# A constant table widened from 49 to 64 floats, so that every later tile in SBUF begins 32 bytes further on

## The chip, the cores and the metric

The kernel runs on one core of a Trainium2 chip. The metric is the device time of one execution in microseconds (us); the time before is the median of three runs. All data are 32-bit floats. The profile is one further execution, taken by the hardware profiler.

The engines are TensorE (PE in the profile; PEld is its loading of weights), VectorE (DVE), ScalarE (ACT), GpSimd (POOL) and SyncE (SP), which here only issues transfers. Transfers run on 16 DMA engines that all queues share.

## The reference

```python
# x: (8, 3136, 256); filt_r, filt_i: (1569, 256)
X = np.fft.rfft(x, axis=1)
Y = X * (filt_r + 1j * filt_i)[None]
y = np.fft.irfft(Y, n=3136, axis=1).astype(np.float32)

h  = y.reshape(25088, 256) @ w_in                  # (25088, 1024)
e  = np.exp(h - np.max(h, axis=-1, keepdims=True))
solu = h * (e / (np.sum(e, axis=-1, keepdims=True) + 1e-9))
mu  = np.mean(solu, axis=-1, keepdims=True)
var = np.mean((solu - mu) ** 2, axis=-1, keepdims=True)
out = ((solu - mu) / np.sqrt(var + 1e-6) * g_ln) @ w_out   # (25088, 256)
```

A filter is applied to each of the 8 batch elements along the sequence by a Fourier transform there and back; then every token goes through a feed-forward block.

## The kernel before

The Fourier transform is made of matrix products in two steps there (49 by 64 points) and two steps back. The last step back uses the table `wb_t`. The intermediate results go through DRAM, since each step needs another order of the rows. Batch element 0 is transformed first; those of elements 1 to 7 run beside the feed-forward blocks of the elements before them.

The constants are allocated one after another, ahead of all working tiles:

```python
wf_t = consts.tile([NR, NK], FP32, name="wf_t")          # 100 floats per partition
wq_t = consts.tile([P, 2, 64], FP32, name="wq_t")        # 128
wi_t = consts.tile([NK, NR], FP32, name="wi_t")          # 98
wb_t = consts.tile([P, N1], FP32, name="wb_t")           # N1 = 49
w_in_sb = consts.tile([P, 7, DFF // 2], FP32, name="w_in_sb")
w_out_sb = consts.tile([P, 7, KF // 2, C // 2], FP32, name="w_out_sb")
...
y = consts.tile([P, KD, PAIR], FP32, name="y")
```

The allocator rounds each tile's bytes per partition up to a multiple of 32. The program before places them so (bytes from the start of a partition):

| tile | begins at | past a multiple of 64 | past a multiple of 512 |
|---|---|---|---|
| wf_t | 16512 | 0 | 128 |
| wq_t | 16928 | 32 | 32 |
| wi_t | 17440 | 32 | 32 |
| wb_t | 17856 | 0 | 448 |
| w_in_sb | 18080 | 32 | 160 |
| w_out_sb | 32416 | 32 | 160 |
| y | 46816 | 32 | 224 |
| turn (two buffers) | 97760, 114144 | 32 | 480 |
| solu_t (four buffers) | 144864 to 157152 | 32 | 480 |
| u, s, h, e, x, t2, t4, f, g, de and the other working tiles | 101856 to 225760 | 32 | 480 |

The small tiles of one to four floats (nmax, esum, rsum and the like) lie 32 bytes apart and alternate between 0 and 32 past a multiple of 64.

The use of the table: 64 products per piece of a batch element, each with a small result of 64 x 49.

```python
def back_halves(e, ch, pss):
    ...
    nc.tensor.matmul(out=views[g][64 * h:64 * h + 64, cb, i, :],        # line 367
                     lhsT=t4[rows, i, c0:c0 + 64], rhs=wb_t[rows],
                     start=True, stop=True)
```

Its load, once: `nc.gpsimd.dma_start(out=wb_t, in_=wb_dram)`.

The feed-forward part works on pairs of blocks of 128 tokens. Each of its two products is done with seven block products in place of eight, from sums and differences of blocks (lines 717 and 829; GpSimd forms the sums, line 696):

```python
nc.tensor.matmul(out=ms[j, bank], lhsT=lhsT, rhs=w_in_sb[:, w, :], ...)          # 717: 128x128 by 128x512
...
for f in range(KF // 2):
    nc.tensor.matmul(out=pos[p, bank], lhsT=lhs[:, f, :], rhs=w[:, f, :], ...)   # 829: 128x128 by 128x128
```

Between the two products the activations must be transposed. VectorE transposes squares of 32 x 32, and transfers from SBUF to SBUF put the squares in place:

```python
def turn(k):
    g, i = divmod(k, 4)
    if i == 0:
        turns[g] = wk2.tile([P, DFF // 32, 4, 32], FP32, name=f"turn_{g}", tag="turn")
    nc.vector.transpose(out=turns[g][:, :, i, :], in_=...)                # line 775

def regroup(p, i):
    turned = turns[g].rearrange("p (k q) b i -> p k q (b i)", q=4)
    a = 2 * second + i
    st = upool.tile([P, KF, P], FP32, name=f"solu_t_{p}_{i}", tag=f"solu_t{i}")
    for q in range(4):
        nc.sync.dma_start(out=st[32 * q:32 * q + 32, :, :],               # line 787
                          in_=turned[32 * a:32 * a + 32, :, q, :])
```

Each of these 784 transfers moves 128 KB from 32 partitions to 32 others, in runs of 512 bytes: 4 x 32 floats that stand together in `turn`, 2048 bytes apart, and go to 8 neighbouring places of 512 bytes in `solu_t`.

Of the kernel before, what the change touches and what calls it, by code (L numbers as in the profile page):

```python
# [9 lines left out]
FP32 = mybir.dt.float32  # L10
# [7 lines left out]
P = 128  # L18
# [5 lines left out]
N1, N2 = 49, 64  # L24
# [70 lines left out]
def kernel(  # L95
# [10 lines left out]
    nc = tc.nc  # L106
# [4 lines left out]
    wb_dram = nc.inline_tensor(wb_host, name="wb_tbl").ap()  # L111
    de_dram = nc.inline_tensor(de_host, name="de_tbl").ap()

    def pool(name, bufs, space=None, stack=ctx):
        kw = {} if space is None else {"space": space}
        return stack.enter_context(tc.tile_pool(name=name, bufs=bufs, **kw))

    consts = pool("consts", 1)
# [8 lines left out]
    wf_t = consts.tile([NR, NK], FP32, name="wf_t")  # L127
    wq_t = consts.tile([P, 2, 64], FP32, name="wq_t")
    wi_t = consts.tile([NK, NR], FP32, name="wi_t")
    wb_t = consts.tile([P, N1], FP32, name="wb_t")  # L130


    w_in_sb = consts.tile([P, 7, DFF // 2], FP32, name="w_in_sb")
# [222 lines left out]
    def back_halves(e, ch, pss):  # L356

        t4 = t4s.pop((e, ch))
        views = [ps.rearrange("p a c -> p (a c)")[:, 0:KD * NCH * N1].rearrange(
            "p (c i r) -> p c i r", c=KD, i=NCH) for ps in pss]  # L360
        for cb in range(KD):
            for i in range(NCH):
                for g in range(2):
                    rows = slice(64 * g, 64 * g + NK // 2)
                    for h in range(2):
                        c0 = cb * P + 64 * h
                        nc.tensor.matmul(out=views[g][64 * h:64 * h + 64, cb, i, :],  # L367
                                         lhsT=t4[rows, i, c0:c0 + 64], rhs=wb_t[rows],
                                         start=True, stop=True)
        even = t4.rearrange("p i c -> p (i c)")[:, 0:KD * NCH * N1]  # L370
        even = even.rearrange("p (c r i) -> p c r i", c=KD, i=NCH)
        nc.scalar.copy(out=even, in_=views[0].rearrange("p c i r -> p c r i"))
        joins[e, ch] = even, views[1].rearrange("p c i r -> p c r i")
# [23 lines left out]
    with ExitStack() as st:  # L397
# [92 lines left out]
        def begin(j):  # L490
            raws[j] = load_words(weights[j][1], j)
# [35 lines left out]
        def idle(out):  # L527

            nc.tensor.matmul(out=out, lhsT=tables[0][0][:, 0, 0].rearrange("p u q -> p (u q)"),
                             rhs=filters[0][0][:, 0], start=True, stop=True)  # L530
# [13 lines left out]
        def start(i):  # L544
            sp.fetch_filter(i)
            sp.fetch_de(i)
            sp.forward(i, halves(f"pb_0_{i}"))
# [4 lines left out]
        for n in range(16):  # L552
            (nc.sync, nc.scalar)[n % 2].dma_start(
                out=t2_0[NH * (n % 4):NH * (n % 4) + NH, n // 4, :], in_=rows_x[n:n + 1])
# [6 lines left out]
        for i in range(units):  # L561
            if i + 2 < units:
                start(i + 2)
            sp.multiply(i, 0, nc.vector.tensor_tensor)
            sp.multiply(i, 1, nc.gpsimd.tensor_tensor)
            pss = [ps_t.tile([P, 2, C], FP32, name=f"pc_0_{i}_{u}", tag="t") for u in range(2)]
            idle(pss[0])
            sp.inverse(i, pss)
            sp.store(i, nc.scalar.dma_start)
            if i == 0:  # L570
                nc.gpsimd.dma_start(out=wi_t, in_=wi_dram)
                nc.gpsimd.dma_start(out=wq_t, in_=wq_dram)
                nc.gpsimd.dma_start(out=wb_t, in_=wb_dram)
                nc.gpsimd.dma_start(out=g_sb, in_=moe_g_ln.rearrange("(k p) -> p k", p=P))
            elif i != 2:
                begin({1: 2, 3: 3, 4: 4, 5: 5, 6: 6}[i])
# [7 lines left out]
        for i0, n, rows in ((0, 4, P), (4, 4, P), (8, NP - 9, P), (NP - 1, 1, NQ)):  # L584
            f, at = filters[i0]
            nc.sync.dma_start(
                out=f_dram[i0:i0 + n].rearrange("i u q k c -> (u q) i (k c)")[0:rows],
                in_=f[0:rows, at:at + n].rearrange("p i k c -> p i (k c)"))
# [279 lines left out]
    for e in range(1, B):  # L868
# [42 lines left out]
        for ch, t in enumerate(back_at):  # L911
            row_loads.append((
                t, t - 1, spectrum_at[-1] + 2, lambda e=e, ch=ch: fetch_back(e, ch)))
            second_one = ch and t == back_at[ch - 1]
            (late if second_one else early)[t].append(lambda e=e, ch=ch: back_halves(
                e, ch, [psum(f"py_{e}_{ch}_{g}") for g in range(2)]))
            (late if second_one else middle)[t].append(lambda e=e, ch=ch: join_halves(e, ch))
# [136 lines left out]
```

## Time and profile before

| | before |
|---|---|
| time, median of 3 runs | 1713.54 us (1708.46 to 1720.54) |
| span of the profiled run | 1710.7 us |
| TensorE busy | 1574.3 us, 92% |
| VectorE busy | 1288.1 us, 75% |
| GpSimd busy | 1139.1 us, 67% |
| ScalarE busy | 904.5 us, 53% |
| moved by DMA | 312.12 MB in 377,805 packets |
| of these on SyncE's queue (q1) | 306,260 packets, 169.81 MB, 47.0% of 16 engines' time |
| packets of 512 bytes (solu_t<-turn) | 200,704, mean 43.3 ns |

How to read it: busy time is that in which an engine has an instruction at work; matrix products are pipelined and their ends are modelled, so a busy TensorE need not be at its peak. The granted clock of TensorE is 0.98 of full speed over the span. The DMA share is the mean of 16 engines. A chain of waits is followed back from the last instruction: at each step to what released it, or to the instruction before it on its engine. The records of single packets have a size, a start and a duration, and no address; the packets of 512 bytes on SyncE's queue are all of the transfer solu_t<-turn, since 784 x 256 = 200,704.

### The profile page before, as it was taken

To read this page: it belongs to the slowest core of one execution; us is meant where nothing else is said; L and a number is where in the kernel's file an instruction comes from. 1 tells how busy PE (TensorE), PEld (TensorE's weight loads), DVE (VectorE), ACT (ScalarE), POOL (GpSimd) and SP (SyncE) were. 2 spreads that over 40 slices of the span, in tenths; PEclk is the share of its full clock that TensorE was granted. 3 is DMA by queue.
4 is the path that set the end of the run, shared out by engine and by line. 5 is a ranking of instruction groups with operands and counts; after the bars stand their busy time and mean duration, and the time that the engine had idled before them with its cause. 6 is when DMAs were issued, how large, how long until landed. Compare 5 with 4: busy or idle time off the path is not lost.

```text
span 1710.7 us, 36871 instructions
## 1 busy us (share of the span) xinstructions
PE 1574.3 (92%) x12710; PEld 1048.9 (61%) x12710; DVE 1288.1 (75%) x2633; ACT 904.5 (53%) x1772; POOL 1139.1 (67%) x1325
## 2 busy tenths in 40 slices
PE   5798899899899999999998999899999999999996
PEld 1353356666656666666665676566666777777776
DVE  1586777887787878887887779777888777777772
ACT  2145454456455555565555654455555565666662
POOL 4444886677766776688567865577757676676664
PEclk8899899999999999999999999999999999999999
DMA  9888878987898779877888779867896666655554
GB/s 248 234 251 233 231 198 200 232 203 178 193 221 215 184 172 225 214 185 168 209 210 206 175 173 210 196 173 166 189 218 172 119 128 123 116 108 103 112 108 96
DMA packets 377805, 312.12 MB, mean 182 GB/s; under 512 B 63322, under 2 KB 343395, under 8 KB 377619
## 3 DMA queue, kind: packets, MB, share of 16 engines
q1 hardware_dynamic: 306260, 169.81, 47.0%
q0 software_dynamic: 34464, 101.68, 21.1%
q10 hardware_dynamic: 36896, 38.28, 8.1%
q8 instruction: 102, 1.67, 0.4%
q14 instruction: 83, 0.68, 0.1%
HBM read 124.86 MB, written 81.50 MB: 121 GB/s over the span
## 4 chain that ended last, share of the span: by engine, by line
PE 54%; DMA 25%; DVE 9%; SPq 4%; issue 4%; ACT 2%; POOL 2%; ACTq 0%; DVEq 0%; POOLq 0%
PE m L717 23%; PE o L829 22%; DMA solu_t<-turn 11%; DMA de<-de_tbl 3%; DMA x<-in_x_dram 3%; SPq L787 3%; PE py L367 3%; DVE h L765 2%; DMA out_dram<-ot 2%; PE pa L221 2%; PE pb L296 1%; DVE turn L775 1%; PE pa L264 1%; DMA rs_t<-rows 1%; PE pc L296 1%
## 5 line engine op out<-in xcount | busy, mean ns | idle before, releaser
L829 PE MATMUL o<-w_out_sb,solu_t 128*128 128x128 f32 x3136 | 402.3, 277 | 38.6 <-DVE rsum L760 36.8
L829 PEld LDWEIGHTS o<-w_out_sb,solu_t 128*128 128x128 f32 x3136 | 380.9, 192 | 89.7 <-DVE rsum L760 43.7
L767 ACT ACTIVATE e<-h,nmu 128x1024 f32<-128x1024 f32 x196 | 224.6, 1146 | 385.6 <-DVE h L765 385.5
L717 PE MATMUL m<-w_in_sb,s 128*128 128x512 f32 x784 | 396.3, 607 | 15.5 <-ACT h L727 13.7
L696 POOL TENSOR_TENSOR u<-solu_t 128x512 f32<-128x512 f32 x98 | 145.4, 1483 | 385.6 <-DMA solu_t<-turn 280.6
L829 PEld LDWEIGHTS o<-w_out_sb,u 128*128 128x128 f32 x2352 | 303.8, 192 | 155.0 <-issue 101.1
L717 PE MATMUL m<-w_in_sb,y 128*128 128x512 f32 x588 | 315.4, 620 | 14.5 <-DVE nmax L741 6.7
L829 PE MATMUL o<-w_out_sb,u 128*128 128x128 f32 x2352 | 315.3, 277 | 9.2 <-ACT ot L841 9.1
L765 DVE SCALAR_TENSOR_TENSOR h<-e,rsum,h 128x1024 f32<-128x1024 f32 x196 | 291.6, 1488 | 6.9
L727 ACT COPY h<-m 128x512 f32<-128x512 f32 x294 | 173.6, 591 | 207.6 <-PE m L717 172.9
L845 DVE SCALAR_TENSOR_TENSOR ot<-o,rs_t,ot 128x128 f32<-128x128 f32 x294 | 100.5, 342 | 199.1 <-ACT ot L841 134.2
L775 DVE STREAM_TRANSPOSE turn<-h 128x1024 f32<-128x1024 f32 x196 | 242.7, 1238 | 0.1
L749 ACT ACTIVATE e<-h,nmax 128x1024 f32<-128x1024 f32 x196 | 226.3, 1155 | 0.0
L741 DVE CUSTOM_DVE_ANT_0 h<-m,h 128x512 f32<-128x512 f32 x196 | 134.7, 687 | 116.8 <-ACT h L727 96.3
L717 PEld LDWEIGHTS m<-w_in_sb,s 128*128 128x128 f32 x784 | 128.3, 191 | 104.1 <-issue 69.4
L841 ACT ACTIVATE ot<-o,rs_t 128x128 f32<-128x128 f32 x392 | 142.9, 365 | 71.8 <-PE o L829 63.3
L696 POOL TENSOR_TENSOR u<-solu_t,u 128x512 f32<-128x512 f32 x98 | 143.2, 1461 | 43.4 <-PE o L829 38.1
L717 PEld LDWEIGHTS m<-w_in_sb,y 128*128 128x128 f32 x588 | 96.8, 193 | 119.7 <-DVE nmax L741 42.2
L696 POOL TENSOR_TENSOR u<-u,solu_t 128x512 f32<-128x512 f32 x98 | 142.3, 1452 | 0.6
L696 POOL TENSOR_TENSOR solu_t<-solu_t,solu_t 128x512 f32<-128x512 f32 x98 | 136.9, 1397 | 7.7
L696 POOL TENSOR_TENSOR s<-y 128x128 f32<-128x128 f32 x196 | 103.8, 530 | 1.0
L367 PEld LDWEIGHTS py<-wb_t,t 50*64 50x64 f32 x3584 | 57.8, 134 | 43.7 <-PE o L829 14.4
(113 smaller groups left out, 1969.6 us busy)
## 6 DMA issues: line engine op xcount, KB each, us to landing
solu_t<-turn SPq DMA_DIRECT2D x784, 128.0 KB
out_dram<-ot SPq DMA_DIRECT2D x196, 128.0 KB
t<-d POOLq DMA_DIRECT2D x112, 200.0 KB, 5.0
d<-x POOLq DMA_DIRECT2D x100, 200.0 KB, 6.4
f<-f_dram POOLq DMA_DIRECT2D x39, 512.0 KB, 8.6
d<-g POOLq DMA_DIRECT2D x39, 512.0 KB, 5.8
t<-d ACTq DMA_DIRECT2D x36, 512.0 KB
x<-in_x_dram SPq DMA_DIRECT2D x112, 98.0 KB
```

What stands on the lines that cost most here:

```text
L367: nc.tensor.matmul(out=views[g][64 * h:64 * h + 64, cb, i, :], lhsT=t4[rows, i, c0:c0 + 64], rhs=wb_t[rows], start=True, stop=True)
L696: nc.gpsimd.tensor_tensor(out=out, in0=in0, in1=in1, op=op)
L717: nc.tensor.matmul(out=ms[j, bank], lhsT=lhsT, rhs=w_in_sb[:, w, :], start=m in (1, 2, 7), stop=True, skip_group_check=True)
L727: nc.scalar.copy(out=h_half(k, i), in_=ms[j, 0])
L741: nc.vector.tensor_tensor_reduce(out=h_half(k, i), in0=ms[j, bank], in1=h_half(*kept), scale=1.0, scalar=sofar, op0=ALU.add, op1=ALU.min, ...
L749: nc.scalar.activation(out=e, in_=hs[k], func=AFT.Exp, bias=nmaxs.pop(k)[:, 1:2], scale=-1.0, accum_out=esum)
L765: nc.vector.scalar_tensor_tensor(out=solu, in0=e, scalar=rsum, in1=solu, op0=ALU.mult, op1=ALU.mult, accum_out=nmu)
L767: nc.scalar.activation(out=e, in_=solu, func=AFT.Square, bias=nmu, scale=-float(DFF), accum_out=variances[g][:, i:i + 1])
L775: nc.vector.transpose(out=turns[g][:, :, i, :], in_=solus.pop(k).rearrange("p (f j) -> p f j", j=32))
L829: nc.tensor.matmul(out=pos[p, bank], lhsT=lhs[:, f, :], rhs=w[:, f, :], start=f == 0 and m in (1, 2, 7), stop=True, skip_group_check=True)
L841: nc.scalar.activation(out=out_half(p, *to)[0], in_=pos[p, 0], func=AFT.Copy, scale=rs)
L845: nc.vector.scalar_tensor_tensor(out=ot, in0=pos[p, bank], scalar=rs, in1=out_half(p, *kept)[0], op0=ALU.mult, op1=ALU.add)
```

## The change

`wb_t` becomes 64 floats wide. The product and the load use the first 49 columns as before. The aim is the place of all that is allocated after it: with 256 bytes in place of 224, every later tile moves up by 32 bytes, so that all large tiles begin at multiples of 64 bytes, and the working tiles, the transposed ones among them, at multiples of 512.

```diff
-    wb_t = consts.tile([P, N1], FP32, name="wb_t")
+    wb_t = consts.tile([P, 64], FP32, name="wb_t")
...
-                                         lhsT=t4[rows, i, c0:c0 + 64], rhs=wb_t[rows],
+                                         lhsT=t4[rows, i, c0:c0 + 64], rhs=wb_t[rows, 0:N1],
                                          start=True, stop=True)
...
-                nc.gpsimd.dma_start(out=wb_t, in_=wb_dram)
+                nc.gpsimd.dma_start(out=wb_t[:, 0:N1], in_=wb_dram)
```

## The prediction

> **What bounds the kernel now.** I read the page's 40 slices first, then the windows by stage, the chain that ended last, the waits, and last the records of single DMA packets. The change moves addresses, and an address is something that a transfer or an engine's operand may feel. The slices say how full TensorE and the transfers are, in tenths:
>
> ```profile
> PE   5798899899899999999998999899999999999996
> DMA  9888878987898779877888779867896666655554
> ```
>
> The windows by stage give the same in microseconds (the columns after the length are PE, PEld, DVE, ACT and POOL busy, then granted clock, DMA share, GB/s):
>
> ```profile
> 200.00:1310.00 1110.00, 1036.54 (x9311) 698.58 (x9311) 895.32 (x1790) 604.94 (x1214) 775.83 (x915) 1.00 0.82 197
> 1310.00:1500.00 190.00, 187.54 (x1526) 133.61 (x1525) 143.19 (x323) 113.52 (x223) 130.99 (x150) 1.00 0.62 123
> 1500.00:1600.00 100.00, 100.00 (x565) 71.54 (x564) 74.45 (x171) 62.48 (x123) 68.91 (x72) 1.00 0.56 108
> ```
>
> So there are two regimes. From 200 to 1310 us the Fourier steps of later batch elements run beside the feed-forward blocks: the 16 DMA engines are 82% busy and TensorE has 1110 - 1036.5 = 73 us of gaps. From 1310 us TensorE is full and the transfers are at 56 to 62%. In that last stage the chain runs through TensorE alone; this is one turn of it, one pair of blocks (14 products of line 717, 56 of line 829, and among the pieces left out the 64 small ones of line 367, 1.08 us):
>
> ```profile
> 1401.89 1.78 PE o L829 x16
> 1403.68 1.72 PE m L717 x4
> 1405.39 1.78 PE o L829 x16
> 1407.18 1.72 PE m L717 x4
> 1408.90 1.78 PE o L829 x16
> ...
> 1415.52 1.78 PE o L829 x16
> ```
>
> It takes 1415.52 - 1401.89 = 13.63 us and nothing but TensorE's own work is in it. No transfer can shorten this stage. The shares of the whole chain, by engine and by line:
>
> ```profile
> PE 54%; DMA 25%; DVE 9%; SPq 4%; issue 4%; ACT 2%; POOL 2%; ACTq 0%; DVEq 0%; POOLq 0%
> PE m L717 23%; PE o L829 22%; DMA solu_t<-turn 11%; DMA de<-de_tbl 3%; DMA x<-in_x_dram 3%; SPq L787 3%; PE py L367 3%; DVE h L765 2%; DMA out_dram<-ot 2%; PE pa L221 2%; PE pb L296 1%; DVE turn L775 1%; PE pa L264 1%; DMA rs_t<-rows 1%; PE pc L296 1%
> ```
>
> And the longest wait for a transfer (us in total, times, longest):
>
> ```profile
> POOL u L696 <- DMA solu_t<-turn: 280.6, 74, 11.0
> ```
>
> The transfer solu_t<-turn (the regrouping of the transposed activations, SBUF to SBUF) is the one that matters: 11.2% of the chain by the unrounded answer, 191 us, its long pieces all before 1310 us, where it stands in a queue with the loads and stores of the Fourier steps. GpSimd waits 280.6 us for it in all, then forms the sums that line 829 multiplies.
>
> [...]
>
> [...] The trace does not show such a penalty plainly. The 16-byte packets of rs_t<-rows read 16-byte rows of which most are off such multiples, and 5,454 of the 6,272 take just 9 ns. And packet times by size (the shortest common value) are 27 ns for 512 bytes, 46 for 1024, 84 for 2048, 159 for 4096: a line of (159 - 46) / 3072 = 0.0368 ns a byte plus 8.3 ns. [...] packets of 4 to 16 bytes take 7 to 9 ns too, so it is rather a fixed cost of any packet.
>
> [...] of the 200,704 packets of 512 bytes, 24% take at most 29 ns and half take 40 to 52 ns, with a median of 44 and a mean of 43.3. [...]
>
> [...]
>
> **The change part by part.** wb_t grows from 49 to 64 floats, from 196 to 256 bytes. The allocator rounds to 32 bytes, so it took 224: everything allocated later moves up by 32 bytes, no more. solu_t goes from 144864 to 144896, which is 283 x 512; turn from 97760 to 97792, 191 x 512; y from 46816 to 46848, 32 past a multiple of 64 to a multiple of 64.
>
> Removed: nothing. Added: nothing. The product of line 367 reads the first 49 of 64 columns in wb_t, one contiguous run as before, so its 3,584 pairs at 134 and about 17 ns stay. The one load of wb_t writes the same rows. No instruction, wait or queue order changes; only what the hardware makes of the addresses can.
>
> The operand that may gain is the 512-byte packet. Its sum is 200,704 x 43.3 ns / 16 engines = 543 us of all engines, of which 361 us fall between 200 and 1310 us, where all packets together take 913. Three outcomes:
>
> (a) No address effect: packets stay at 43.3 ns, nothing moves. Time 1713 plus or minus the spread of the runs (1708.46 to 1720.54).
>
> (b) A small effect: [...] a saving of 3 to 4 ns is plausible, 8% (chosen, not derived). On the path: 8% of the chain's 191 us = 15 us. Elsewhere: 8% of 361 = 29 us less work of 913 in the shared stage, 3%, which shortens the queueing of the other chained transfers (25% of 1711 = 428 us, less 191, is 237 us) by up to 3%, 7 us. Of the 22 us I expect part to be lost, since TensorE takes over wherever it catches up: some 15 us. Time about 1698.
>
> (c) The full estimate: each packet falls to near its floor, 43.3 to 31 ns, 28%. On the path 0.28 x 191 = 53 us; the others 0.28 x 361 / 913 = 11% of 237 = 26 us. Together 79, but TensorE has only 73 us of gaps in the shared stage and not all belong to this wait; perhaps 50 us with what the start gives. Time about 1663.
>
> **The rivals.** Rival one is (a), that 32 past a multiple of 64 costs nothing: for it speak the 9 ns packets, the line through the sizes[...]. [...] Rival two: the transfers do get faster but the end does not, because TensorE is the bound. For it: 92% busy, and the last 400 us run on TensorE alone. Against: GpSimd's 280.6 us of waiting and 25% of the chain in transfers before 1310 us. It would put the time at 1705 to 1713. Rival three: the engines feel 64-byte lines, GpSimd above all, since its sums of 128x512 take 1277 ns (median of u<-solu_t) and hold VectorE up (line 765 takes 1285 ns at the median and up to 2510). A few per cent off these would be worth 5 to 10 us. Nothing in the profile speaks for it but the round number. Rival four, slower: all work tiles now start at the same place within 512 bytes, but they did before too, at 480, so I see no new collision; a changed order of arrivals may cost a few microseconds.
>
> **Range and chances.** I give (a) with rivals two to four 55%, centred on 1712; (b) 33%, on 1698; (c) 12%, on 1663. The mean is 0.55 x 1712 + 0.33 x 1698 + 0.12 x 1663 = 1701.5; the middle of the distribution lies a little higher, so I say 1704. Faster by over 2% means below 1679.3: nearly all of (c) and a little of (b), 0.16. Slower by over 2%, above 1747.8, has no mechanism: 0.03. The rest, 0.81, within 2%. Eight times in ten: 1670 to 1720.
>
> **What would show it.** Right: the 512-byte packets' mean at 39 to 43 ns, DMA share between 200 and 1310 us at 0.79 to 0.82, the wait of GpSimd for solu_t<-turn at 250 to 280 us, and the late turn at 13.63 us still. If packets fall below 35 ns, (c) holds and the DMA share should drop to about 0.73. If packets stay and GpSimd's 1277 ns or TensorE's 13.63 us change, it was the engines' side. [...]

## The result and the profile after

The kernel after takes 1694.69 us (median of 4 runs, 1693.12 to 1697.80), the kernel before 1713.92 beside it. The ratio is 0.9888, 95% interval 0.985 to 0.9926: 1.1% faster.

The slices of the kernel after, TensorE and transfers:

```profile
PE   5897899999989999999989999999999999999996
DMA  9886868776788678666886668766883544344343
```

and its windows, with the same columns as before:

```profile
200.00:1310.00 1110.00, 1055.35 (x9448) 715.07 (x9449) 909.47 (x1837) 618.69 (x1241) 788.85 (x934) 1.00 0.73 199
1310.00:1500.00 190.00, 182.57 (x1476) 129.74 (x1475) 141.80 (x305) 110.41 (x216) 124.14 (x141) 1.00 0.45 113
1500.00:1600.00 100.00, 96.59 (x544) 68.70 (x543) 76.29 (x166) 59.68 (x117) 64.56 (x68) 1.00 0.41 104
```

Two things happened. Up to 1310 us the DMA share fell from 0.82 to 0.73 while slightly more bytes were moved per second (197 to 199 GB/s), and TensorE's gaps shrank from 73 to 55 us. After 1310 us the transfers have even more room (0.62 to 0.45, 0.56 to 0.41), and there TensorE, full before, now has gaps: 2.5 us of 190 became 7.4, and 0 of 100 became 3.4.

The packets of 512 bytes (all of solu_t<-turn) went from a mean of 43.3 to 33.0 ns. GpSimd's wait for that transfer, 280.6 us before, and the chain of the kernel after:

```profile
POOL u L696 <- DMA solu_t<-turn: 146.2, 43, 7.7
```

```profile
PE 53%; DMA 19%; DVE 15%; issue 4%; POOL 4%; SPq 3%; ACT 1%; ACTq 0%; DVEq 0%; POOLq 0%
```

Transfers fell from 25% of the chain to 19%, but VectorE rose from 9% to 15%. Where that sits is seen in the chain of the kernel after in the last stage, which before was TensorE alone (start, length, what):

```profile
1500.50 1.16 DVE turn L775
...
1502.19 2.38 DVE h L765 x2
1504.57 0.68 DVE h L738 x2
...
1505.30 1.13 PE m L717 x2
1506.42 0.95 PE o L829 x8
```

In most turns TensorE now waits for VectorE: for line 738, which empties the PSUM bank that the next product needs and which stands behind a line 765 of 2.38 us with its accumulator read. The waits from 1310 to 1600 us (us in total, times, longest), first of the kernel before, then of the kernel after:

```profile
PE m L717 <- DVE h L738: 1.1, 2, 0.7
```

```profile
PE m L717 <- DVE h L738: 10.8, 17, 0.9
```

A clock for both kernels is the start of chosen products of line 717 in the profiled runs (1372 products of 128x512 in all; numbers count from 0):

| | first product, us | from there to product 980 | from 980 to the last | rest | span |
|---|---|---|---|---|---|
| before | 113.7 | 1186.1 | 362.2 | 48.8 | 1710.7 |
| after | 107.7 | 1157.4 | 380.0 | 50.9 | 1695.9 |
| difference | -6.1 | -28.7 | +17.8 | +2.1 | -14.8 |

So 35 us were gained by product 980 and 18 given back after it. The third column is called the shared stage below, the fourth the last stage.

### The profile page after: what moved, and what is told of

Read it like the earlier page. It is cut to its first block, busy times and chain, and to the rows that moved or that the text cites. A ratio compares the mean times of both kernels' runs of the same rounds, so it can differ in the third digit from the quotient of the medians.

```text
span 1695.9 us, 36871 instructions
## 1 busy us (share of the span) xinstructions
PE 1568.3 (92%) x12710; PEld 1050.2 (62%) x12710; DVE 1299.2 (77%) x2633; ACT 904.1 (53%) x1772; POOL 1136.0 (67%) x1325
## 4 chain that ended last, share of the span: by engine, by line
PE 53%; DMA 19%; DVE 15%; issue 4%; POOL 4%; SPq 3%; ACT 1%; ACTq 0%; DVEq 0%; POOLq 0%
PE m L717 21%; PE o L829 21%; DMA solu_t<-turn 11%; DVE h L765 5%; PE py L367 3%; DVE turn L775 3%; SPq L787 3%; PE pb L296 2%; PE pa L264 2%; DMA x<-in_x_dram 2%; DVE h L738 2%; PE pc L296 1%; DVE ot L845 1%; DMA d<-x 1%; DMA rows<-rs 1%
## 5 line engine op out<-in xcount | busy, mean ns | idle before, releaser
L696 POOL TENSOR_TENSOR u<-solu_t 128x512 f32<-128x512 f32 x98 | 131.7, 1344 | 308.1 <-DMA solu_t<-turn 146.2
L765 DVE SCALAR_TENSOR_TENSOR h<-e,rsum,h 128x1024 f32<-128x1024 f32 x196 | 302.3, 1542 | 6.9
L741 DVE CUSTOM_DVE_ANT_0 h<-m,h 128x512 f32<-128x512 f32 x196 | 134.8, 688 | 113.7 <-ACT h L727 93.0
L717 PEld LDWEIGHTS m<-w_in_sb,y 128*128 128x128 f32 x588 | 96.0, 191 | 128.7 <-DVE h L738 44.5
L696 POOL TENSOR_TENSOR solu_t<-solu_t,solu_t 128x512 f32<-128x512 f32 x98 | 153.4, 1565 | 7.7
L367 PEld LDWEIGHTS py<-wb_t,t 50*64 50x64 f32 x3584 | 57.6, 134 | 42.9 <-PE o L829 14.4
```

The source lines that it names most:

```text
L696: nc.gpsimd.tensor_tensor(out=out, in0=in0, in1=in1, op=op)
L741: nc.vector.tensor_tensor_reduce(out=h_half(k, i), in0=ms[j, bank], in1=h_half(*kept), scale=1.0, scalar=sofar, op0=ALU.add, op1=ALU.min, ...
L765: nc.vector.scalar_tensor_tensor(out=solu, in0=e, scalar=rsum, in1=solu, op0=ALU.mult, op1=ALU.mult, accum_out=nmu)
```

## The experiments

All were timed beside the kernel before, whose medians in the three sets were 1717.20, 1716.43 and 1717.07 us; the ratios refer to these. "Shared" packets are those of 512 bytes between 200 and 1250 us, "late" ones those from 1400 us on. For these two, and for the start of product 980 in experiments 9 and 10, time counts from the trace's zero, which lies 10.4 to 10.8 us ahead of the span's start; all other times count from the span's start. Shared stage and last stage are as in the table above, from one profile each. The three profiles in which nothing but GpSimd's own tiles or the order of late sums differs from the kernel before agree within 6.3 us in the shared stage (1183.4 to 1189.7), so a difference of a few microseconds between two profiles there is not read.

### 1. src_only: the destination off its place again

```diff
 # the kernel after
+    pad_a = pool("pad_a", 1).tile([P, 8], FP32, name="pad_a")
     upool = pool("up", 2)
+    pad_b = pool("pad_b", 1).tile([P, 120], FP32, name="pad_b")
```

> The kernel after, but solu_t (and u1, s14 beside it) 32 bytes further on: the source turn still starts at a multiple of 512, the destination solu_t is 32 past one. Theory R (the read side pays[...]): packets of 512 bytes stay at 33 ns as in the kernel after, time about 1695 us. Theory W (the write side pays[...]): packets go back to 43 ns, time about 1713. Theory L (both ends pay alike): about 38 ns, time about 1700.

Measured: 1708.33 us, ratio 0.9951 (0.9928 to 0.9974). Packets 35.4 ns in all, 36.5 shared, 32.3 late (after: 33.0, 33.3, 32.1). Shared stage 1165.0, last stage 378.7. The read end sets the late packets: with the source in place they take 32.1 ns with the destination in place too and 32.3 with it off. Where the transfers are busier (DMA share 0.77 from 200 to 1250 us in this run, 0.42 from 1400 to 1600) the write end shows too, 36.5 for 33.3.

### 2. dst_only: the destination alone in its place

```diff
 # the kernel before, with the same two pads
+    pad_a = pool("pad_a", 1).tile([P, 8], FP32, name="pad_a")
     upool = pool("up", 2)
+    pad_b = pool("pad_b", 1).tile([P, 120], FP32, name="pad_b")
```

> The kernel before, but solu_t (and u1, s14 beside it) 32 bytes further on: the destination starts at a multiple of 512, the source turn stays at 480 past one. Theory R: packets stay at 43 ns, time about 1713 us. Theory W: packets fall to 33 ns, time about 1695. Theory L: about 38 ns, time about 1703.

Measured: 1695.48 us, ratio 0.9877 (0.9843 to 0.9912). Packets 41.6 in all, 40.5 shared, 44.3 late (before: 43.3, 42.9, 44.6). Theory R was right on the packets (they hardly change) and wrong on the time: the whole 1.2% is there. Shared stage 1165.8, and the last stage stays at 362.4, as in the kernel before. So the time does not follow the packets of this transfer.

### 3. past64 and past256: which multiple matters

```diff
-    wb_t = consts.tile([P, 64], FP32, name="wb_t")
+    wb_t = consts.tile([P, 80], FP32, name="wb_t")     # past64; 128 for past256
```

> The kernel after with the table 80 floats wide: every later tile 64 bytes further on, so turn and solu_t are 64 past a multiple of 512: a multiple of 64, not of 256. If multiples of 64 are what matters: packets 33 ns, time 1695 us, no difference from the kernel after. If multiples of 256 or 512 matter[...]: 36 to 43 ns, time 1700 to 1713.

> The kernel after with the table 128 floats wide: every later tile 256 bytes further on, so turn and solu_t are 256 past a multiple of 512. If multiples of 64 or of 256 are what matters: packets 33 ns, time 1695 us. If a run may not cross a multiple of 512: 38 to 43 ns, time 1705 to 1713.

Measured: past64 1706.38 us, ratio 0.9924 (0.9886 to 0.9963), packets 37.3 in all and 36.0 late, shared stage 1177.3, last 363.4. past256 1694.25 us, ratio 0.9858 (0.9824 to 0.9892), packets 33.1 and 32.2, shared stage 1153.6, last 377.9. A multiple of 64 is not enough, and 512 is not needed; a multiple of 256 does all that the change does.

### 4. after_wait_late: why the last stage became slower

VectorE's line 765 (the normalising product) and GpSimd's sums of line 696 start near each other in every turn. In the kernel before (timeline, start and length in us):

```profile
1550.87 1.28 DVE L765 SCALAR_TENSOR_TENSOR h<-e,rsum,h 128x1024 f32<-128x1024 f32 x1
1551.22 2.07 POOL L696 TENSOR_TENSOR u<-solu_t 128x512 f32<-128x512 f32 x1 [2.45 <-DMA solu_t<-turn]
```

and in the kernel after:

```profile
1528.75 1.27 POOL L696 TENSOR_TENSOR u<-solu_t 128x512 f32<-128x512 f32 x1 [1.88 <-DMA solu_t<-turn]
1528.98 2.11 DVE L765 SCALAR_TENSOR_TENSOR h<-e,rsum,h 128x1024 f32<-128x1024 f32 x1
1530.09 2.14 POOL L696 TENSOR_TENSOR solu_t<-solu_t,solu_t 128x512 f32<-128x512 f32 x1
```

Whichever starts first runs at its own length, 1.27 or 1.28 us, and the other is stretched by about the rest of it. In the 14 profiles the turning point lies at 0.05 us: all 188 sums u<-solu_t that start between 0.85 us before line 765 and 0.05 us after it leave line 765 stretched, to between 1.52 and 2.42 us, and all 243 that start 0.05 to 0.85 us after it are stretched themselves, to between 1.57 and 2.37. (In the chain shown above line 765 starts at 1502.19, the sum at 1502.22, and line 765 is the stretched one.) Before, solu_t landed so late that GpSimd was the one to wait, which cost nothing. After, it lands a little earlier, GpSimd starts 0.23 us ahead of line 765 here (by the median from 1310 to 1600 us 0.21 us ahead, where it was 0.34 us behind), and VectorE is held up. It is as if line 765 began only when the sum had ended, to 0.2 us: the sum ends at 1530.02, plus 1.28 is 1531.30 (an estimate from these lengths), and line 765 ends at 1531.09. What the two instructions share was not shown. A stretched line 765 is frequent in that stage: from 1310 us on, 22 of the kernel after's 52 lines 765 take over 1.5 us, and 20 of them start while u<-solu_t runs; before it was 4 of 57, and 2 of them.

```diff
 # the kernel after; cond is 144 <= k < blocks
             if 0 <= j - 3 < pairs:
-                project_sums(j - 3, 0)
+                if not (cond):
+                    project_sums(j - 3, 0)
...
-            normalize(k - 2)
+            nmu = normalize(k - 2)           # returns line 765's column of sums
+            if odd and 0 <= j - 3 < pairs and (cond):
+                seen = small.tile([P, 64], FP32, name=f"seen_{k}", tag="seen", bufs=2)
+                nc.gpsimd.tensor_copy(out=seen[:, 0:1], in_=nmu)
+                project_sums(j - 3, 0)
```

> The kernel after; for the blocks from k = 144 on (roughly the last 400 us) GpSimd's two sums that follow the landing of solu_t are put behind a copy of one column of the normalising instruction's output (line 765), so that they cannot start while VectorE is about to run or running it. Theory C (the gain is given back in the last stage because the earlier landing puts GpSimd's sum just ahead of line 765[...]): the last 392 products of line 717 take about 362 us as in the kernel before, not 380, line 765 there falls from a mean of 1614 ns to about 1330, time 1695 - 17 = about 1678 us. Rival T (TensorE is slower there for a reason of its own, addresses or clock): no change, about 1695 us. Rival D (the extra copy and the later sums starve TensorE): slower, 1700 us or more.

Measured: 1678.65 us, ratio 0.9788 (0.9746 to 0.9831). Last stage 364.6, line 765 there at a mean of 1424 ns (after: 1614). The pair in its timeline:

```profile
1501.47 1.28 DVE L765 SCALAR_TENSOR_TENSOR h<-e,rsum,h 128x1024 f32<-128x1024 f32 x1
...
1503.00 1.27 POOL L696 TENSOR_TENSOR u<-solu_t 128x512 f32<-128x512 f32 x1
```

Theory C holds, in place and in size (1678 expected). Line 765 did not fall quite to 1330: 15 are still over 1.5 us, 13 of them beside another sum, u<-u,solu_t, and the stage is as short as before all the same: not every stretched line 765 reaches TensorE. What does is the wait for line 738: over the last stage TensorE's products of line 717 waited for it 1.1 us before, 14.0 after and 1.3 with this edit.

### 5. before_wait_late: the same edit without the change

The diff is that of experiment 4, on the kernel before.

> The same edit on the kernel before, where the sum already starts after line 765 in that stage. Theory C: nothing to win, 1710 to 1720 us, the last 392 products at about 362 us. Rival T: nothing either. If the edit itself makes the last stage faster whatever the addresses: under 1705 us.

Measured: 1714.97 us, ratio 0.9993 (0.9975 to 1.0011), shared stage 1183.4, last stage 363.3. The edit brings nothing by itself; it only removes what the change had broken.

### 6. u_only: a control of experiment 2

```diff
 # the kernel before; solu_t in a pool of its own, left at 480
+    tpool = pool("tpool", 2)
+    pad_a = pool("pad_a", 1).tile([P, 8], FP32, name="pad_a")
     upool = pool("up", 2)
+    pad_b = pool("pad_b", 1).tile([P, 120], FP32, name="pad_b")
...
-        st = upool.tile([P, KF, P], FP32, ...)
+        st = tpool.tile([P, KF, P], FP32, ...)
```

> The control of the run in which the destination alone was moved: the kernel before with u1 and s14 (written by GpSimd, moved there too) at multiples of 512, and solu_t left at 480 past one. If the write end of the transfer made that run 1.2% faster: here nothing, 1712 to 1720 us. If it was the place of GpSimd's own tiles, or chance in the order of events: about 1696 us.

Measured: 1712.88 us, ratio 0.9978 (0.9955 to 1.0002), shared stage 1189.7, last 361.8. The place of GpSimd's own tiles does nothing; in experiment 2 it was the place of solu_t.

### 7. others_only and others_480: all but the regrouping transfer in place

```diff
 # the kernel after; turn and solu_t each in a pool of its own, with a pad before and after it
+    pad_a = pool("pad_a", 1).tile([P, 8], FP32, name="pad_a")        # 120 in others_480
+    turn_pool = pool("turn_pool", 2)
+    pad_b = pool("pad_b", 1).tile([P, 120], FP32, name="pad_b")      # 8 in others_480
     wk2 = pool("wk2", 2)
...
     upool = pool("up", 2)
+    pad_c = pool("pad_c", 1).tile([P, 8], FP32, name="pad_c")        # 120
+    tpool = pool("tpool", 2)
+    pad_d = pool("pad_d", 1).tile([P, 120], FP32, name="pad_d")      # 8
...                          # the two tiles then come from turn_pool and tpool
```

> The kernel after with turn and solu_t alone moved 32 bytes off their multiples of 512; all other tiles stay at multiples of 64 (512 for the working tiles). If the two ends of the regrouping transfer carry the whole gain: packets of 512 bytes back at 43 ns, time 1712 to 1718 us as in the kernel before. If the loads and stores of the Fourier steps or the engines' operands gain from the place as well: 1700 to 1708 us.

> As the run in which turn and solu_t alone were moved off, but back to exactly the 480 past a multiple of 512 of the kernel before; everything else stays at multiples of 64. If the two ends of the regrouping transfer carry the whole gain: packets of 512 bytes at 43 ns (44.6 from 1400 us on), time 1710 to 1718 us as before. If the loads and stores of the Fourier steps and the engines' operands gain as well: 1700 to 1708 us.

Measured: others_only 1694.72 us, ratio 0.988 (0.9837 to 0.9922), but it was no clean test: at 32 past a multiple of 512 the late packets take 35.5 ns, not the 44.6 of 480 past. others_480 puts both ends exactly where they were: 1698.07 us (1683.79 to 1706.58), ratio 0.9873 (0.9813 to 0.9933), with packets at 43.3 ns in all, 43.0 shared and 44.5 late, nothing of the transfer regained. The queue's line of the kernel after, and that of others_480:

```profile
q1 hardware_dynamic: 306260, 169.81, 39.0%
```

```profile
q1 hardware_dynamic: 306260, 169.81, 47.2%
```

The second is the 47.0% of the kernel before, and yet the time is within its uncertainty that of the kernel after. Shared stage 1167.4, last stage 361.1, TensorE full again from 1400 to 1600 us. So the place of the other tiles alone is worth about 1.3%, since nothing is given back in the last stage.

### 8. src128: does the packet grow evenly with the source's distance from a multiple of 256

```diff
 # the kernel after; turn in a pool of its own
+    pad_a = pool("pad_a", 1).tile([P, 32], FP32, name="pad_a")
+    turn_pool = pool("turn_pool", 2)
+    pad_b = pool("pad_b", 1).tile([P, 96], FP32, name="pad_b")
...                          # turn then comes from turn_pool
```

> The kernel after with turn alone at 128 past a multiple of 512. [...] on the line through the starts measured[...] that is 39.5 ns there. If only the distance to a multiple of 64[...] mattered: 36 ns, as for 64 past.

Measured, in a single run: 1697.62 us, late packets 35.8 ns, as for 64 past, not 39.5. So they do not grow evenly: by the place alone, a straight line from 36.0 ns at 64 past to 44.6 at 224 gives 39.4 at 128, an estimate from these two. Late packets by the source's place past a multiple of 256: 0, 32.1 to 32.3 ns; 32, 64 and 128, 35.5 to 36.0; 224, 44.3 to 44.6. Why 224 is so much worse than the rest is open; the places between 128 and 224 were not tried.

The stages of this run tell more: 1158.0 and 379.1 us, both those of the kernel after, though its late packets are as long as those of others_only and past64, whose last stages take 361.2 and 363.4. So the loss in the last stage does not follow the mean packet. It follows the landing: from 1310 to 1600 us the 1024 packets of one solu_t tile pass in 2.8 us (median, first start to last end) in after, past256, src_only, dst64 and src128, where 15 to 18 of 21 sums start before line 765 or less than 0.05 us after it and the last stage takes 377.9 to 380.4. In before, u_only, dst_only, others_480, others_only and past64 they pass in 3.2 to 3.5 us, at most 3 of some 22 sums start so early, and the stage takes 361.1 to 363.4.

### 9. dst64: what the write end minds

```diff
 # the kernel after; solu_t in a pool of its own
+    pad_c = pool("pad_c", 1).tile([P, 16], FP32, name="pad_c")
+    tpool = pool("tpool", 2)
+    pad_d = pool("pad_d", 1).tile([P, 112], FP32, name="pad_d")
...                          # solu_t then comes from tpool
```

> The kernel after with solu_t alone at 64 past a multiple of 512. If the write end suffers from lines of 64 bytes only partly filled: no loss, 33.3 ns for the packets of 512 bytes between 200 and 1250 us, product 980 of line 717 at about 1275 us. If it suffers from runs that cross multiples of 256: as with 32 past, 36.5 ns and about 1287 us.

Measured: 1704.85 us, ratio 0.9929 (0.9904 to 0.9954), packets 35.7 shared and 32.3 late, product 980 at 1286.9 us. As with 32 past (src_only, 36.5 shared): a destination at a multiple of 64 is no better. At a multiple of 512 (after) the shared packets take 33.3; with both ends at one of 256 (past256) the packets are 33.1 ns in all, the kernel after's 33.0.

### 10. after_wait_all: the order set in all blocks

The diff of experiment 4 with the condition `k < blocks`.

> The kernel after with GpSimd's two sums behind the normalising instruction in all blocks, not only from k = 144 on. If the collision on line 765 costs as much in the shared stage (44 of 138 are stretched there): product 980 earlier than 1271 us and the time under 1674 us. If the shared stage is held up by transfers and the sums are late as it is: later than 1275 us, and 1680 us or more.

Measured: 1671.33 us, ratio 0.9736 (0.9696 to 0.9776) to the kernel before; product 980 at 1266.5 us, both under the bounds expected; last stage 363.0. Its waits of GpSimd between 200 and 1275 us, the new one for line 765 and the old one for the transfer:

```profile
POOL seen L1007 <- DVE h L765: 177.7, 61, 4.9
POOL u L696 <- DMA solu_t<-turn: 34.0, 18, 5.3
```

and its chain:

```profile
PE 62%; DMA 15%; DVE 11%; issue 4%; POOL 3%; SPq 2%; ACT 2%; DVEq 0%; ACTq 0%; POOLq 0%
```

In the same stretch of the kernel before GpSimd waited 192.5 us for the transfer. Now it waits for VectorE by design, while the transfer lands. Up to product 980 line 765 is stretched over 1.5 us 37 times of 138 (44 in the kernel after), its mean 1485 ns in place of 1504. TensorE's part of the chain rises from 54 to 62%. The kernel after was not run beside it; the two ratios to the kernel before, 0.9888 and 0.9736, put it 1.5% ahead. The same order in all blocks of the kernel before was not tried, so how much of this it would gain without the change is not known.

## Why the prediction was right in the time and wrong in its reasons

**The time.** 1694.69 lies in the range of 1670 to 1720, below the 1704 that was said and closest to outcome (b), 1698; outcome (a) with its rivals, 1712, had been given 55%. That it is so near (b) is luck: the packets gained what (c) says, tiles that the prediction did not count on gained some 20 us, and 18 us were given back in a stage that it held to be out of reach. The signs that it named for being right failed: packets at 33.0 ns for 39 to 43, the DMA share at 0.73 for 0.79 to 0.82, GpSimd's wait at 146.2 us for 250 to 280.

**"32 past a multiple of 64 costs nothing: for it speak the 9 ns packets, the line through the sizes".** This step failed. The same transfers, between the same partitions as before, have packets of 33.3 ns in the shared stage and 32.1 late when the source starts at a multiple of 256 (experiments 1, 3), and 8% of all packets take 40 to 52 ns where half did. So most of the slow packets went with the address. The line was drawn through the most frequent times, and the most frequent time of 512 bytes is 27 ns in either kernel, so the packets at that floor could not show it. Nor could the 9 ns packets of rs_t<-rows, which read rows in DRAM and not in SBUF. The boundary that counts here is 256 (experiment 3); what sets the sizes was not shown (experiment 8).

**"3 to 4 ns is plausible, 8% (chosen, not derived)."** The term was mis-sized: 10.3 ns, 24%, nearly outcome (c)'s 28%. The DMA share in the shared stage fell to 0.73, the very figure that the prediction gave for (c).

**"28% ... perhaps 50 us."** With packets of (c) the time should have been about 1663. The conversion from packets to time failed twice. The second failure, the last stage, is the next point. The first: "The operand that may gain is the 512-byte packet" was wrong. Against the 1186.1 us of the kernel before, the shared stage takes:

| in place (a multiple of 256) | shared stage, us | late packets, ns |
|---|---|---|
| nothing (before; u_only) | 1186.1; 1189.7 | 44.6; 44.4 |
| destination of the transfer (dst_only) | 1165.8 | 44.3 |
| all but the transfer (others_480) | 1167.4 | 44.5 |
| all but the destination (src_only, where u1 and s14 are off too; dst64) | 1165.0, 1166.7 | 32.3, 32.3 |
| all but the source, which is at 128 (src128) | 1158.0 | 35.8 |
| everything (after, past256) | 1157.4, 1153.6 | 32.1, 32.2 |

The destination and the other tiles bring some 20 us each; all three parts together bring 29 to 33, less than the sum of these two. The source, which alone shortens the packets much, adds little to the other tiles: 1 to 2 us by these profiles, though that of others_480 was of its fastest run; by the medians, less what the last stage loses, 1698.07 against 1708.33 - 16.5 = 1692 and 1704.85 - 18.2 = 1687, an estimate of 6 to 11. With the source at 128 the stage is as short as with everything in place. The prediction took 191 us of chain as if it were transfer time to be scaled. In the kernel after, with packets 24% shorter, solu_t<-turn still has 11.0% of the chain, 187 us; and in u_only and before_wait_late, with the packets and the time of the kernel before, it has 8.5% and 7.0%. So the chain's share was not a sum that the packets' length scales. (Two of its sums, 361 and 913 us, count from the trace's zero; from the span's start they are 365 and 911, which changes nothing.)

**"No transfer can shorten this stage", "the late turn at 13.63 us still".** It cannot shorten it, but it can lengthen it: 362.2 became 380.0. The prediction saw that GpSimd "holds VectorE up" and did not ask what an earlier landing would start. Rival two, that TensorE takes over, was not it either: the last stage lost to a new wait, which experiments 4, 5 and 8 show. With that wait gone the change is worth 1678.65, 2.1%.

**Held.** The engines do not feel the address: medians of line 829 275 ns, line 717 592, line 765 1285 and 1286, u<-solu_t 1277 and 1273, before and after. Rival three falls with it. No run shows a loss to a new collision of addresses.

**Open.** Why the other tiles, or solu_t as destination alone, are worth 20 us. Packets of other queues are a little shorter in both cases: those of 1024 bytes on ScalarE's queue, 61.6 ns in the shared stage before, take 58.1 in dst_only and 56.4 in others_480, but 61.3 in u_only; the landing of d<-x is 6.4 us before, 5.8 and 5.6 in these two and 6.1 in u_only. What connects these packets with the place of the other tiles was not shown. The source alone in place, and everything in place but the source at 224, were not tried; nor is it known which of the other tiles count.

## What to carry to other kernels

Try tiles that transfers read or write in pieces at multiples of 256 bytes, the destination and the tiles of ordinary loads and stores as well as the obvious strided source (here the destination alone and the other tiles alone were each worth some 20 us of 1186), and judge it by the stage's time, not by the packets. A transfer's share of the chain is not time that shrinks with its packets (11% for solu_t<-turn before and after, with packets 24% shorter). Before a transfer is made faster, look at what its landing releases: an engine that starts earlier can stretch the instruction of one that was on time (line 765 from 1.28 us to as much as 2.42 here), and then the order has to be set by hand (1678.65 us in place of 1694.69 here).

## What the runs showed of the hardware that was not expected

The length of the 512-byte packets from SBUF to SBUF follows the start of the source in three steps, from 1400 us on: 32 ns at a multiple of 256, 36 at 32, 64 and 128 past it, 44.5 at 224 past. A destination off its place is not seen from 1400 us on (32.3 ns off, 32.1 in place; 44.6 off, 44.3 in place), only in the shared stage (36.5 off, 33.3 in place). And which of GpSimd's sum and VectorE's line 765 starts first, to 0.05 us, decides which of them is up to 1.1 us longer; over the last stage that was worth 18 us.
